# A late row block rectified by ScalarE, an input sum one step later, indirect stores through two views

## The chip, the cores and the metric

One core of a Trainium2 chip runs the whole program. Five engines work side by side, each through its own queue of instructions in a fixed order: TensorE (PE, with its weight loads as PEld), VectorE (DVE), ScalarE (ACT), GpSimd (POOL) and SyncE (SP, which only issues transfers here). An instruction waits at the head of its engine's queue until what it needs is done, and everything behind it in that queue waits too. The metric is device time of one execution in microseconds.

## The reference

An attention with decay over blocks of 64 rows feeds a Fourier mixing block with a feed-forward layer. Cut to what matters:

```python
# q, k, v: (4, 8, 768, 64); lam: (8,)
for b in range(nb):                                   # blocks of 64 rows
    intra = einsum('bhic,bhjc->bhij', qb, kb) * Dmask
    out[:, :, sl] = einsum('bhij,bhjd->bhid', intra, vb) + einsum('bhid,bhde->bhie', qb * lam_pow, kv_state)
    kv_state = lam ** 64 * kv_state + einsum('bhsd,bhse->bhde', kb * rev_pow, vb)
x = out.transpose(0, 2, 1, 3).reshape(4, 768, 512)

u = x + real(fft(fft(x, axis=1), axis=2))
un = (u - mean(u)) / sqrt(var(u) + 1e-6)              # over the last axis
return u + maximum(un @ w_ch1, 0.0) @ w_ch2           # w_ch1 512 x 2048, w_ch2 2048 x 512
```

All of it is float32. The change lies in the last line, the feed-forward layer, and in the writing of its result.

## The kernel before

**Stages.** The first part of the program computes attention, the transforms and the normalisation, batch by batch, and weaves the feed-forward layer of the first row groups into it. A row group is 256 rows of a batch; there are twelve. The first four (`PLAIN`) are multiplied plainly (`mlp`). The other eight (`LATE`) wait in DRAM and are done at the end, from 409 us of the profile on, as four pairs of groups.

**A pair.** The two matrix products of a pair are done by a scheme of seven products of half-size blocks in place of eight, with sums of blocks before and after (`PRODUCTS` lists the seven: a11·b11, a12·b21, s3·t3, s2·t2, s1·t1, a22·t4, s4·b22; a is of the weights, b of the inputs, s and t are sums). Before the pairs begin, `combine_weights` makes the sums of the weights. Most products are split once more into seven (`seven`, `deep_first`, `deep_second`). The first layer of the first pair alone is split only once: that is `first_layer(0)`. After it come the first pair's second layer and the other three pairs; `in_step` interleaves the last products of one pair with the first ones of the next, so the beginning of pair j+1 runs beside the end of pair j.

**`first_layer`.** It runs over eight blocks i of 128 hidden units. Each has seven products of four matmul instructions each (line 1031), gathered in three banks of PSUM, X, Y and Z:

- `begin(i)`: a11·b11 into X, copied out by ScalarE (line 1052); a12·b21 into Y, added by VectorE (line 1054) and rectified by it (line 1055). This runs up to three blocks ahead.
- the loop: s2·t2 is added into X, and ScalarE copies it to a12 (line 1069); s3·t3 goes into Z; s1·t1 is added into X, ScalarE copies it to a22 (line 1072), VectorE adds Z (line 1073) and rectifies (line 1074).
- `finish` of the block before, called "late" below: s4·b22 is added into X, and ScalarE rectifies that into a21 (line 1041); a22·t4 is added into Z, VectorE adds it to a12 (line 1043) and rectifies a12 (line 1044); then VectorE forms the sums a21 + a22 and a11 - a21 for the second layer (lines 1045 and 1046).

The engines' queues don't follow the text of the code exactly: a scheduler sets their order, apart from instructions pinned by `keep_in_program_order`. In VectorE's queue a late block's lines come as 1045, 1046, 1043, 1044, and the rectified a12 is read only by the second layer. Meanwhile GpSimd forms 28 sums of the second layer's weights, four for each of seven products (`keep_sums`, lines 855 and 859), and SP stores three of each four in DRAM.

**`inputs`.** For pairs 1 to 3 this generator makes the sums of the inputs that the deep first layer needs. It starts with line 941 (B12 = B22 - B12, pinned in program order), which reads what `load_u` (line 894, issued by SP) brings in. `in_step` takes a step of it in turn with a step of the products around it; each `yield` ends a step. On VectorE these sums lie among the additions of the second layer of the pair before (line 1206).

**`store`.** Results of the upper half of a batch's rows come out in reversed order, so they are written by an indirect transfer that GpSimd issues (line 738), with row numbers from the table `ix`. The lower half is written by SP (line 736). `dram_disjoint_views` tells the framework that two views of the output don't overlap, so that it orders no write in one after a write in the other; writes through one view are ordered one after another, each waiting for the one before to land.

Of the kernel before, what the change touches and what calls it, by code (L numbers as in the profile page):

```python
# [16 lines left out]
AF = mybir.ActivationFunctionType  # L17
ALU = mybir.AluOpType
# [59 lines left out]
def kernel(  # L78
# [10 lines left out]
    nc = tc.nc  # L89
# [50 lines left out]
    def new(pool, shape, tag, **kw):  # L140
        cnt[0] += 1
        return pool.tile(shape, F32, tag=tag, name=f"{tag}{cnt[0]}", **kw)
# [43 lines left out]
    def row_of(j, n=128):  # L186
        return bass.IndirectOffsetOnAxis(ap=ix[0:n, j:j + 1], axis=0)
# [540 lines left out]
    ORDER = [(b, g) for b in range(B) for g in (1, 2, 0)]  # L728
    PLAIN, LATE = ORDER[:4], ORDER[4:]

    out_low, out_high = dram_disjoint_views(out.rearrange("b s d -> (b s) d"), 2)

    def store(b, T, y, cols=slice(0, DM)):
        if T < HC:
            row = S * b + 128 * T
            nc.sync.dma_start(out_low[row:row + 128, cols], y[:, cols])
        else:
            nc.gpsimd.indirect_dma_start(out=out_high,
                                         out_offset=row_of(2 + HC * (b + 1) + T - HC),
                                         in_=y[:, :], in_offset=None)  # L740

# [67 lines left out]
    V = nc.vector  # L809
# [41 lines left out]
    def keep_sums(k):  # L851

        pin = tc.keep_in_program_order
        B11, B12, B21, B22 = quarters_b(s2.B[PRODUCTS[k][1]])
        pin(nc.gpsimd.tensor_tensor(B12, B22, B12, op=SUB))
        T1, T2, T4 = t = [new(s2.yp, [128, HF // 2, HM // 2], "tx", bufs=6) for _ in range(3)]
        s2.td.append([dram.tile([128, HF // 2, HM // 2], F32, name=f"td{k}{i}") for i in range(3)])
        for i, o, x, y, op in ((1, T2, B12, B11, ADD), (0, T1, B22, T2, SUB), (2, T4, B21, T2, SUB)):
            pin(nc.gpsimd.tensor_tensor(o, x, y, op=op))
            nc.sync.dma_start(s2.td[k][i], o)  # L860
# [37 lines left out]
    def bank():  # L898
        return new(s2.ps, [128, DM], "p2")
# [18 lines left out]
    def inputs(j):  # L918

        P, r = pairs[j], s2.u.pop(j)  # L920
        b11, b21, b12, b22 = r[:, 0, 0:2], r[:, 0, 2:4], r[:, 1, 0:2], r[:, 1, 2:4]

        def sx(shape):
            return new(s2.hp, shape, "sx", bufs=6)

        P.U = U = dict(b11=b11, b21=b21, b22=b22, t3=b12)
        if j < DEEP:
            U["t1"], U["t2"], U["t4"] = t1, t2, t4 = [sx([128, 2, G * 128]) for _ in range(3)]
            V.tensor_tensor(t1, b12, b11, op=SUB)
            yield 0.0  # L930
            V.tensor_tensor(t2, b22, t1, op=SUB)
            yield 0.0
            V.tensor_tensor(t4, b21, t2, op=SUB)
            yield 0.0
            V.tensor_tensor(b12, b22, b12, op=SUB)
            yield 0.0
            return


        B11, B12, B21, B22 = (r[:, :, k::2, m:m + 128] for k in range(2) for m in (0, 128))  # L940
        tc.keep_in_program_order(V.tensor_tensor(B12, B22, B12, op=SUB))
        yield 0.0
        t1 = U["t1"] = sx([128, 2, G * 128])
        V.tensor_tensor(t1, b12, b11, op=SUB)
        yield 0.0
        V.tensor_tensor(b12, b22, b12, op=SUB)
        yield 0.0
        T2, T1, T4 = [sx([128, 2, 2, 128]) for _ in range(3)]
        V.tensor_tensor(T2, B12, B11, op=ADD)
        yield 0.0  # L950
        V.tensor_tensor(T1, B22, T2, op=SUB)
        yield 0.0
        V.tensor_tensor(T4, B21, T2, op=SUB)
        yield 0.0
        P.T = {n: [t[:, h, k] for t in (T1, T2, T4)]
               for n, h, k in (("b11", 0, 0), ("b21", 0, 1), ("t3", 1, 0), ("b22", 1, 1))}
        t2, t4 = U["t2"], U["t4"] = [sx([128, 2, G * 128]) for _ in range(2)]
        V.tensor_tensor(t2, b22, t1, op=SUB)
        yield 0.0
        q2, q1, q4 = [new(s2.hp, [128, 3, 128], "sv", bufs=3) for _ in range(3)]  # L960
        for i, n in enumerate(("t2", "t1", "t4")):
            C11, C12, C21, C22 = (U[n][:, k, m:m + 128] for k in range(2) for m in (0, 128))
            if n == "t4":
                nc.gpsimd.tensor_tensor(t4, b21, t2, op=SUB)
                yield 0.0
            nc.gpsimd.tensor_tensor(q2[:, i], C12, C11, op=ADD)
            nc.gpsimd.tensor_tensor(q1[:, i], C22, q2[:, i], op=SUB)
            nc.gpsimd.tensor_tensor(q4[:, i], C21, q2[:, i], op=SUB)
            P.T[n] = [q1[:, i], q2[:, i], q4[:, i]]
            yield 0.0  # L970
# [10 lines left out]
    def load_x(j):  # L981
        P = pairs[j]
        P.us = [new(s2.yp, [128, G, DM], "u2", bufs=2) for _ in range(2)]
        for k in range(2):
            for s in range(G):
                tc.keep_in_program_order(nc.sync.dma_start(P.us[k][:, s], ud[P.who[k][s]]))

    def open_y(j):
        P = pairs[j]
        P.yt = new(s2.yp, [128, 2, G, DM], "y2")  # L990
        P.y = [P.yt[:, k, :, m:m + HM] for k in range(2) for m in (0, HM)]

    def split(t):

        A11, _, A21, _ = quarters_a(t)
        tc.keep_in_program_order(V.tensor_tensor(A21, A11, A21, op=SUB))
# [20 lines left out]
    def prepare_b(j, k):  # L1017
        t = yield from load_three(k, s2.td)
        pairs[j].pre_b[k] = [x.rearrange("p (a b) -> p a b", a=HF // 2) for x in t]
# [4 lines left out]
    def first_layer(j):  # L1024

        P = pairs[j]
        h, U = P.h, P.U

        def prod(ps, a, b, i, first):
            for kt in range(2):  # L1030
                nc.tensor.matmul(ps, lhsT=s2.A[a][:, kt, 128 * i:128 * i + 128], rhs=U[b][:, kt, :],  # L1031
                                 start=(first and kt == 0), stop=(kt == 1), skip_group_check=True)

        def two(t):
            return t.rearrange("p (s k) -> p s k", s=G)

        def finish(i, X, Z):
            a11, a12, a22, s1, s3 = (h[n][:, :, i, :] for n in ("a11", "a12", "a22", "s1", "s3"))
            prod(X, "s4", "b22", i, False)
            a21 = new(s2.hp, [128, G, 128], "sv", bufs=3)  # L1040
            nc.scalar.activation(a21, two(X), AF.Relu)
            prod(Z, "a22", "t4", i, False)
            V.tensor_tensor(a12, two(Z), a12, op=ADD)
            V.tensor_scalar(a12, a12, 0.0, None, op0=ALU.max)
            V.tensor_tensor(s1, a21, a22, op=ADD)
            V.tensor_tensor(s3, a11, a21, op=SUB)

        def begin(i):
            a11 = h["a11"][:, :, i, :]
            X, Y = (bank()[:, 0:G * 128] for _ in range(2))  # L1050
            prod(X, "a11", "b11", i, True)
            nc.scalar.copy(a11, two(X))
            prod(Y, "a12", "b21", i, True)
            V.tensor_tensor(a11, two(Y), a11, op=ADD)
            V.tensor_scalar(a11, a11, 0.0, None, op0=ALU.max)
            return X

        last = None
        AHEAD = 3
        begun = [begin(i) for i in range(AHEAD)]  # L1060
        for i in range(HF):
            a12, a22 = (h[n][:, :, i, :] for n in ("a12", "a22"))
            if i >= AHEAD:
                begun.append(begin(i))
            X, Z = begun[i], bank()[:, 0:G * 128]
            if last:
                finish(*last)
            prod(X, "s2", "t2", i, False)
            nc.scalar.copy(a12, two(X))
            prod(Z, "s3", "t3", i, True)  # L1070
            prod(X, "s1", "t1", i, False)
            nc.scalar.copy(a22, two(X))
            V.tensor_tensor(a22, two(Z), a22, op=ADD)
            V.tensor_scalar(a22, a22, 0.0, None, op0=ALU.max)
            last = (i, X, Z)
            if i < len(PRODUCTS):
                if i == 0:
                    tc.keep_in_program_order(nc.gpsimd.tensor_copy(s2.begun, h["a11"][:, 0, 0, 0:1]))
                keep_sums(i)
            if i == HF - 3:  # L1080
                load_x(j)
            if i == HF - 2:
                for k in range(2):
                    run(prepare_b(j, k))
            if i > HF // 2:
                split(h[("a11", "a12", "s3")[i - HF // 2 - 1]])
        run(prepare_a(j, 0))
        finish(*last)
        run(prepare_a(j, 1))
        open_y(j)  # L1090
# [263 lines left out]
    def run(gen):  # L1354
        return sum(gen)
# [82 lines left out]
```

## Time and profile before

| What | us |
|---|---|
| median of 3 runs | 777.26 |
| lowest and highest run | 775.27, 777.77 |
| profiled execution, its own time | 773.78 |
| its span in the profile | 771.7 |
| stage of `first_layer`, from its first to its last matmul | 409.6 to 461 |
| pairs from there to the last matmul | 461 to 767 |

| Stretch, us | PE busy | VectorE busy | ScalarE busy | GpSimd busy |
|---|---|---|---|---|
| 409 to 420 (11) | 10.97 | 8.54 | 2.62 | 6.50 |
| 440 to 450 (10) | 10.00 | 9.82 | 2.36 | 9.76 |
| 450 to 460 (10) | 10.00 | 9.76 | 2.63 | 3.30 |
| 460 to 498 (38) | 38.00 | 32.72 | 4.25 | 8.99 |
| 498 to 546 (48) | 47.43 | 42.75 | 16.55 | 12.96 |
| 722 to 771.7 (49.7) | 44.86 | 35.42 | 5.88 | 8.31 |

A row of a timeline gives start and length in us, engine, line, operation, the tile written and the tiles read, and in brackets how long the engine stood idle before it and for whom. Tile names are cut to letters: `p` is a bank of PSUM, `ha` stands for a11, a12 and a22, `hs` for s1 and s3, `sv` for a21, `sx`, `tx` and `ur` for inputs and their sums. One row can hold several instructions (x4). An instruction that has to wait for more than a queue's own order often shows as a longer duration, not as idle time: an operation of VectorE on 128x256 elements has a median of 0.91 us at line 1044 and a least value of 0.29.

### The profile page before, as it was taken

Reading aid. Unit: us, or ns where it says so; the run is one execution under the profiler, and the core shown is the slowest. Engines: PE = TensorE matmul, PEld = TensorE weight load, DVE = VectorE, ACT = ScalarE, POOL = GpSimd, SP = SyncE. Lnnn points to the kernel's source line nnn. Section 1 sums busy time; section 2 is a strip of 40 time slices with the busy share of each in tenths; the row PEclk is TensorE's granted clock in tenths of the full one; section 3 lists DMA queues with packets and bytes.
Section 4 is the critical chain, followed back from the end, with each engine's and each line's share of the span. In section 5 each row is a group of like instructions: output and inputs, shape, how many; then the busy total and the mean of one; then the engine's idle time right before and its main releaser. Section 6 shows DMA issues by size and latency. Waiting matters only on the chain.

```text
span 771.7 us, 15006 instructions
## 1 busy us (share of the span) xinstructions
PE 752.6 (98%) x5784; PEld 646.7 (84%) x5784; DVE 602.8 (78%) x1167; ACT 231.1 (30%) x532; POOL 178.4 (23%) x202
## 2 busy tenths in 40 slices
PE   6989999999999999999999999999999999999997
PEld 5777877777685967769747899999999999999997
DVE  6999998784936575336898999788986699758984
ACT  3755443435521221322101221034301341024310
POOL 3223330021111113220105941360015001230013
PEclk9999999999999999999999999999999999999999
DMA  9979732347943149731433465876545456455442
GB/s 240 274 161 250 195 125 86 106 96 181 246 117 94 45 82 270 176 97 35 113 65 124 150 218 164 273 234 202 180 124 178 125 186 182 127 175 180 144 141 70
DMA packets 154924, 120.22 MB, mean 156 GB/s; under 512 B 114286, under 2 KB 116974, under 8 KB 154854
## 3 DMA queue, kind: packets, MB, share of 16 engines
q1 hardware_dynamic: 147792, 100.51, 46.7%
q0 software_dynamic: 4032, 12.99, 4.7%
q10 hardware_dynamic: 3030, 5.78, 2.1%
q8 instruction: 46, 0.75, 0.4%
q14 instruction: 24, 0.20, 0.1%
HBM read 88.04 MB, written 31.20 MB: 155 GB/s over the span
## 4 chain that ended last, share of the span: by engine, by line
PE 88%; DVE 7%; DMA 2%; ACT 1%; issue 1%; POOL 0%; SPq 0%; DVEq 0%; ACTq 0%
PE p L1198 22%; PE p L1124 17%; PE pm L763 13%; PE pm L749 13%; PE p L1031 6%; PE pa L603 3%; PE pa L379 3%; PE pa L338 3%; PE pa L373 2%; PE pa L314 1%; PE pa L358 1%; PE pa L395 1%; DVE sc L343 1%; PE pa L763 1%; PE pa L319 1%
## 5 line engine op out<-in xcount | busy, mean ns | idle before, releaser
L749 PE MATMUL pm<-ut,w 128*128 128x256 f32 x512 | 118.3, 381 | 0.0
L763 PE MATMUL pm<-w,hr 128*128 128x512 f32 x240 | 108.7, 596 | 0.1
L749 PEld LDWEIGHTS pm<-ut,w 128*128 128x128 f32 x512 | 94.7, 190 | 14.4 <-issue 2.7
L763 PEld LDWEIGHTS pm<-w,hr 128*128 128x128 f32 x240 | 43.8, 190 | 45.5 <-issue 43.8
L1219 POOL TENSOR_TENSOR y<-y,u 128x512 f32<-128x512 f32 x12 | 19.9, 1661 | 186.8 <-DVE y L1228 155.5
L1198 PE MATMUL p<-tx,sx 128*128 128x128 f32 x400 | 52.7, 275 | 0.0
L1198 PEld LDWEIGHTS p<-tx,sx 128*128 128x128 f32 x400 | 48.6, 192 | 0.0
L1133 DVE TENSOR_TENSOR ha<-p,ha 128x512 f32<-128x512 f32 x60 | 40.1, 686 | 8.6 <-PE p L1124 8.6
L1204 ACT COPY y<-p 128x128 f32<-128x128 f32 x48 | 12.8, 266 | 103.6 <-PE p L1198 103.1
L310 POOL TENSOR_TENSOR kd<-k,decay 128x512 f32<-128x512 f32 x20 | 21.7, 1083 | 86.5 <-PE pa L358 50.1
L343 DVE TENSOR_TENSOR sc<-pa,decay 128x512 f32<-128x512 f32 x48 | 30.9, 683 | 11.7 <-PE pa L338 11.5
L1206 DVE TENSOR_TENSOR y<-p,y 128x128 f32<-128x128 f32 x92 | 25.6, 285 | 15.6 <-PE p L1198 9.1
L1198 PE MATMUL p<-w,ha 128*128 128x128 f32 x288 | 37.4, 275 | 0.0
L1133 DVE TENSOR_TENSOR hs<-p,hs 128x512 f32<-128x512 f32 x39 | 26.2, 685 | 12.4 <-PE p L1124 12.4
L338 PEld LDWEIGHTS pa<-qT,kT 64*128 64x128 f32 x384 | 25.1, 193 | 12.2 <-ACT qT L321 6.4
L1198 PEld LDWEIGHTS p<-w,ha 128*128 128x128 f32 x288 | 34.9, 192 | 0.1
L638 POOL TENSOR_SCALAR ve<-mv 128x2 f32<-128x2 f32 x12 | 6.2, 519 | 120.0 <-DVE mv L635 120.0
L757 ACT ACTIVATE hr<-pm 128x256 f32<-128x256 f32 x44 | 16.7, 382 | 57.6 <-PE pm L749 53.7
L1124 PE MATMUL p<-sx,tx 128*128 128x128 f32 x264 | 33.9, 275 | 0.0
L338 PE MATMUL pa<-qT,kT 64*128 64x128 f32 x384 | 30.1, 292 | 2.9 <-ACT qT L321 2.9
L1124 PEld LDWEIGHTS p<-sx,tx 128*128 128x128 f32 x264 | 31.7, 192 | 0.0
L379 PE MATMUL pa<-sc,v 128*64 128x128 f32 x384 | 28.9, 282 | 1.3 <-DVE sc L343 1.0
(274 smaller groups left out, 1748.4 us busy)
## 6 DMA issues: line engine op xcount, KB each, us to landing
tx<-td SPq DMA_DIRECT2D x84, 256.0 KB, 2.9
raw<-in_moe_w_ch_dram SPq DMA_DIRECT2D x32, 512.0 KB, 4.3
tx<-sd SPq DMA_DIRECT2D x63, 256.0 KB, 2.8
k<-in_k_dram SPq DMA_DIRECT2D x24, 256.0 KB, 3.7
q<-in_q_dram SPq DMA_DIRECT2D x24, 256.0 KB, 7.0
v<-in_v_dram SPq DMA_DIRECT2D x24, 256.0 KB, 5.7
td<-tx SPq DMA_DIRECT2D x21, 256.0 KB, 2.0
ud<-x SPq DMA_DIRECT2D x16, 256.0 KB, 3.1
```

What stands on the lines that cost most here:

```text
L310: nc.gpsimd.tensor_tensor(kd, kt, kpow, op=ALU.mult)
L338: mm(pss[hi][:, hp, :], lhsT=kT[HD[hi], hp, :], rhs=qT[HD[hi], hp, :], start=True, stop=True)
L343: nc.vector.tensor_tensor(t, pss[hi], decay[:, hi::2, :], op=ALU.mult)
L379: mm(po[HD[hi], hp, :], lhsT=vt[:, 2 * hp + hi, :], rhs=sc[hi][:, hp, :], start=(c == 0 and hp == 0), stop=(hp == HP - 1), skip_group_chec ...
L603: mm = nc.tensor.matmul(ps[:, n, :], lhsT=piece(a, i, n), rhs=cs[0:rows, a, i in (2, 3), n, :], start=(a == 0), stop=(a == 1))
L749: nc.tensor.matmul(ps, lhsT=w1[:, c, 128 * fc:128 * fc + 128], rhs=ut[:, c, :], start=(c == 0), stop=(c == KO - 1))
L763: return nc.tensor.matmul(ps, lhsT=hr[(fc - f0) // 4][:, fc % 4, 128 * i:128 * i + 128], rhs=w2[:, fc, :], start=(fc == f0), stop=(fc == f ...
L1031: nc.tensor.matmul(ps, lhsT=s2.A[a][:, kt, 128 * i:128 * i + 128], rhs=U[b][:, kt, :], start=(first and kt == 0), stop=(kt == 1), skip_gro ...
L1124: nc.tensor.matmul(ps[:, 128 * i:128 * i + 128], lhsT=ab[m][0][:, 128 * i:128 * i + 128], rhs=ab[m][1], start=(start and i == 0), stop=Tru ...
L1133: V.tensor_tensor(o, p, o, op=ADD)
L1198: nc.tensor.matmul(ps[:, 0:HM // 2], lhsT=ab[m][0][i], rhs=ab[m][1][:, i, :], start=(start and i == 0), stop=(i == HF // 2 - 1), skip_grou ...
L1206: V.tensor_tensor(o, ps[:, 0:HM // 2], o, op=ADD)
```

## The change

It has three parts. The rectifying of a12 in `finish` is written as an activation of ScalarE instead of a VectorE operation; it is done for eight blocks. In `inputs`, for the pairs from the second on, a `yield` stands ahead of the first sum, so that sum is formed one step later. The output is declared as three views that don't overlap, one for SP's stores and two for the indirect stores, which use the two in turns.

```diff
-    out_low, out_high = dram_disjoint_views(out.rearrange("b s d -> (b s) d"), 2)
+    out_low, *out_high = dram_disjoint_views(out.rearrange("b s d -> (b s) d"), 3)
+    uppers = [0]
 
     def store(b, T, y, cols=slice(0, DM)):
         if T < HC:
             row = S * b + 128 * T
             nc.sync.dma_start(out_low[row:row + 128, cols], y[:, cols])
         else:
-            nc.gpsimd.indirect_dma_start(out=out_high,
+            uppers[0] += 1
+            nc.gpsimd.indirect_dma_start(out=out_high[uppers[0] % 2],
                                          out_offset=row_of(2 + HC * (b + 1) + T - HC),
                                          in_=y[:, :], in_offset=None)
...
         B11, B12, B21, B22 = (r[:, :, k::2, m:m + 128] for k in range(2) for m in (0, 128))
+        yield 0.0
         tc.keep_in_program_order(V.tensor_tensor(B12, B22, B12, op=SUB))
...
             prod(Z, "a22", "t4", i, False)
             V.tensor_tensor(a12, two(Z), a12, op=ADD)
-            V.tensor_scalar(a12, a12, 0.0, None, op0=ALU.max)
+            nc.scalar.activation(a12, a12, AF.Relu)
             V.tensor_tensor(s1, a21, a22, op=ADD)
             V.tensor_tensor(s3, a11, a21, op=SUB)
```

## The prediction

> **What bounds the kernel now.** I read the page first, for the engine that fills the span, then busy time by stretch, for where that engine has holes, then its waits, then the order of time around each hole.
>
> ```profile
> span 771.7 us, 15006 instructions
> PE 752.6 (98%) x5784; PEld 646.7 (84%) x5784; DVE 602.8 (78%) x1167; ACT 231.1 (30%) x532; POOL 178.4 (23%) x202
> ```
>
> PE is busy 98% of the span, so an edit counts only where PE stands still. Busy time by stretch (columns: stretch, length, then PE, PEld, DVE, ACT, POOL busy, granted clock, DMA share, GB/s) and PE's waits after 409 us (total, times, longest):
>
> ```profile
> 420.00:430.00 10.00, 9.24 (x43) 7.57 (x41) 9.67 (x13) 1.87 (x5) 9.69 (x8) 1.00 0.38 141
> 430.00:440.00 10.00, 10.00 (x48) 8.81 (x48) 9.82 (x15) 2.52 (x7) 9.69 (x8) 1.00 0.36 133
> ```
> ```profile
> PE p L1031 <- DVE ha L1073: 0.8, 1, 0.8
> PE p L1198 <- DVE y L1206: 0.6, 1, 0.6
> ```
>
> Between 409 us and the last matmul these two holes, 0.76 and 0.57 us, are all that an edit could give back there: 1.33 us. The clock is 1.00, so nothing is to be had from it either. The stage of the first edit (`first_layer`, 409 to 461 us) is special in another way: VectorE is 98% busy there too, and GpSimd 97%. Five starts of products on PE, and what the other engines do meanwhile (start, length):
>
> ```profile
> 435.22 1.03 PE L1031 MATMUL p<-ur,w1s 128*128 128x256 f32 x4
> 436.08 1.03 PE L1031 MATMUL p<-sx,w 128*128 128x256 f32 x4
> 436.95 1.03 PE L1031 MATMUL p<-sx,w1s 128*128 128x256 f32 x4
> 437.81 1.03 PE L1031 MATMUL p<-ur,w 128*128 128x256 f32 x4
> 438.67 1.03 PE L1031 MATMUL p<-sx,w1s 128*128 128x256 f32 x4
> ```
> ```profile
> 436.33 0.38 ACT L1041 ACTIVATE sv<-p 128x256 f32<-128x256 f32 x1 [1.40 <-PE p L1031]
> 437.60 0.41 DVE L1045 TENSOR_TENSOR hs<-sv,ha 128x256 f32<-128x256 f32 x1
> 437.60 1.53 POOL L859 TENSOR_TENSOR tx<-w2s 128x512 f32<-128x512 f32 x1
> 437.93 1.49 DVE L1046 TENSOR_TENSOR hs<-ha,sv 128x256 f32<-128x256 f32 x1
> 438.01 0.37 ACT L1069 COPY ha<-p 128x256 f32<-128x256 f32 x1 [1.29 <-PE p L1031]
> 439.34 0.41 DVE L1043 TENSOR_TENSOR ha<-p,ha 128x256 f32<-128x256 f32 x1
> 439.79 0.91 DVE L1044 TENSOR_SCALAR ha<-ha 128x256 f32<-128x256 f32 x1
> 439.74 0.37 ACT L1072 COPY ha<-p 128x256 f32<-128x256 f32 x1 [1.35 <-PE p L1031]
> ```
>
> The products are, in order, s4·b22 and a22·t4 of the late block, then s2·t2, s3·t3, s1·t1 of the current one, 0.86 us apart. L1043 adds a22·t4, which PE had issued by 436.95, but starts at 439.34: VectorE runs 2.4 us behind PE. That harms nothing, since no instruction that PE waits for stands behind L1043 closely enough. Three VectorE operations whose operands all lie in SBUF (L1044, L1046, L1074) end shortly after a GpSimd sum does: L1044 takes 0.29 us at 461.05, when GpSimd is silent, and 0.91 us here.
>
> **Edit 1, the rectifying of the late block.** It takes L1044 off VectorE, 8 times: six of 0.91 and two of 0.29 us, 6.0 us of work. It puts 8 Relu activations on ScalarE; L1041 is the same shape there, 0.38 us, so 3.1 us on an engine 25% busy. By work alone this is a relief. The wait is the matter. The Relu waits for L1043, and in ScalarE's queue it stands, from block 3 on, directly after L1041 and ahead of L1069, the copy of s2·t2. PE may add s1·t1 to that bank only after that copy. For blocks 1 and 2 it stands ahead of L1072, which s4·b22 needs. So VectorE's lateness, harmless till now, reaches PE.
>
> The Trainium skill ("ScalarE: Activation LUTs", Rules for kernel authors) says to do relu on VectorE rather than ScalarE; its reason is the rate per element. Here the rows say otherwise on the rate (0.91 against 0.38), and by the rule's reason alone the stage would lose nothing, since ScalarE has room; it is the queue order that costs.
>
> The chain from the end of s4·b22 to s1·t1, by rows: to L1041's start 0.25 (436.08 to 436.33), L1041 0.38, on to VectorE 0.04, then x, the time from L1045's start to L1043's, then L1043 0.41, on to ScalarE 0.07 (L1054 ends 442.31, L1041 starts 442.38), Relu 0.38, copy L1069 0.37, on to PE 0.05. Without x that is 1.95. PE has three products to do meanwhile, 3 x 0.86 = 2.58. So x may be 0.63. The rows of x: 0.67 and 0.68 at 456.10 and 459.92, when GpSimd had finished; 1.74 at 432.02 and 437.60 (L1046 held by one GpSimd sum); 2.65 and 2.63 at 420.18 and 425.56 (L1045 held as well). PE therefore loses 0.04, 1.1 or 2.0 us per block.
>
> Block by block. Blocks 1 and 2: the first L1043 ends at 423.24, as no L1044 precedes it; Relu to 423.69, L1072 to 424.06 (it ended at 422.50), s4·b22 starts at 424.11 instead of 422.79. L1073 then runs at 424.13 (424.11 before), so a22·t4 follows at 424.97 instead of 424.57: the old hole of 0.76 is spent in this, and 0.4 is lost. Block 2 gives 0.1 of it back: 0.3. Block 3: VectorE still has L1074, L1054 and L1055 ahead of L1045, and reaches it at 431.95, about as now (432.02), 1.1 us after a21 is ready; L1043 ends at 434.1, Relu and copy at 434.9, s1·t1 starts at 434.97 where it was due at 432.8: 2.2. Blocks 4 and 5: VectorE, lighter by L1044, is no longer late, and x decides; the rows show both kinds, so one of 2.0 and one of 1.1. Blocks 6 and 7: GpSimd, which waits for none of this, is through at 453.4 or a little earlier; L1045 of block 6 would come at 454.5 on the delayed PE: 0.1 for both. Sum: 0.3 + 2.2 + 3.1 + 0.1 = 5.7 us lost. Bounds: 1.1 for each of blocks 3 to 5 and nothing else, 3.3; 2.2, 2.0, 2.0, 2.0 (block 6 too) with 0.4 and 0.3 around them, 8.9.
>
> The skill ("SBUF — State Buffer", Who interferes with whom) holds that a VectorE operation with two SBUF inputs, or in a two-port mode, and a GpSimd operation shut each other out for a whole instruction, and that ScalarE waits on nobody. The rows above agree for VectorE; by that rule alone edit 1 frees 6 x 0.6 us of blocked time and the sum would be a gain of at most the 0.76 us hole.
>
> **Edit 2, the first input sum one step later.** L941 now stands in VectorE's queue after one more L1206.
>
> ```profile
> 498.54 0.69 DVE L941 TENSOR_TENSOR ur<-ur 128x512 f32<-128x512 f32 x1 [2.70 <-DMA ur<-utd]
> 499.15 0.28 DVE L1206 TENSOR_TENSOR y<-p,y 128x128 f32<-128x128 f32 x1
> 499.49 0.97 PEld L1198 LDWEIGHTS p<-w2s,sx 128*128 128x128 f32 x8 [0.76 <-DVE y L1206]
> ```
>
> VectorE waits 2.7 us for the transfer of the second pair's inputs, and the L1206 behind it holds PE 0.57 us. That L1206 goes ahead now. Behind L941 stand another L1206 and the sums; the first that PE takes (L949, 501.24 to 501.91) is used at 504.95, 3.0 us later, or 2.4 once PE is earlier. So -0.57; bounds -0.57 and 0 (if the next L1206 becomes the one that holds). At 585 and 671 us L941 waits for nothing: 0. No DMA is issued by it, and SP's order is the same.
>
> **Edit 3, two views.** Each indirect store no longer waits for the previous one to land, but for the one before that. The rows of this line's semaphore waits give 17 ns at the least, 43 in the middle and 3026 at the most; the one long wait runs from 761.9 us, for the last store.
>
> ```profile
> 762.11 0.98 POOL L738 DMA_INDIRECT out_dram<-y,ix  x1 [5.50 <-DVE y L1206]
> 765.63 0.97 POOL L738 DMA_INDIRECT out_dram<-y,ix  x1 [2.54 <-DVE y L1206]
> ```
>
> That wait ends near 764.9, and VectorE delivers y only at 765.40, so the store starts when it did. It lands 2.9 us later, near 768.5, while the span ends at 771.7 with SP's last stores (issued at 767.2). 0; if that cover were gone, 0.7 us off a path that doesn't end the span. GpSimd's other waits are longer than any landing.
>
> **The sum.** 5.7 - 0.57 = +5.1 us, on 773.78 us of the profiled execution (span 771.7 and 2.1 around it): 778.9. The median shown is 777.26, 3.5 above that execution; I put the change on the median: 782.4.
>
> **Rivals.** (a) *Relief wins.* In `first_layer`, if VectorE, lighter by 0.91 a block, keeps x at or under 0.63, the Relu is always ready in time; PE keeps both holes' 1.33 us: 775.9. For it: VectorE 98% busy. Against it: 0.67 even with GpSimd silent, and GpSimd is busy till 453. The point is x = 0.63. This is within 0.3% (2.3 us, what a measurement can tell from no change); beyond that no hole is left to fill. (b) *One hold per block*: 3.3 - 0.57 = +2.7: 780.0. For it: four of the six early rows of x are near 1.74. Against: block 3's queue. (c) *Two holds per block through block 6, and edit 2 gives nothing*: +8.9: 786.2. For it: the two rows with L1045 held too, and VectorE's queue in block 3. Against: GpSimd ends early. (d) *An edit that doesn't do what it says*: the second view takes a wait away that VectorE covers, so the stores start as before. I hold this to be so, and it is part of every case.
>
> **How the numbers follow.** Forecast (+3.5 to +7.5) 0.56; (b) 0.17; (c) 0.13; (a) 0.14, of which 0.03 is faster by over 0.3% (a mistake of mine in the holes) and 0.11 within it. (b) at +2.7 lies just beyond 0.3%, so 0.02 of it goes to no change. Slower 0.84, same 0.13, faster 0.03. The range runs from 778.5 (below (b), by the scatter of 1 to 2 us in the runs) to 787.3 (past (c)).
>
> **What would show it.** Right: PE waiting in 420 to 452 us for ScalarE's L1069 and L1072, some 5 us in all; ScalarE waiting for L1043 ahead of each Relu; VectorE with idle time there; L1206 no longer behind L941's wait, and PE without its hole at the start of the second pair; second-last wait of L738 gone with the same end. Wrong: PE unbroken through 420 to 450, or L1045 and L1046 near 0.4 us there; or a new hole behind L941.

## The result, and the profile after

| | median, us | lowest and highest | runs |
|---|---|---|---|
| before | 775.98 | 775.27, 777.77 | 6 |
| changed | 779.95 | 778.45, 782.08 | 6 |

The changed kernel takes 1.0049 of the time of before, 95% interval 1.003 to 1.0067: about 3.8 us slower, where +5.1 was forecast. The page of its profiled execution begins:

```profile
span 779.9 us, 15013 instructions
PE 753.6 (97%) x5784; PEld 646.5 (83%) x5784; DVE 595.8 (76%) x1159; ACT 233.2 (30%) x540; POOL 177.1 (23%) x202
```

VectorE is busy 7.0 us less than before (602.8), ScalarE 2.1 us more (231.1): the work moved as the diff says. But the two spans can't be subtracted. The first matmul of line 603, long before any of the edits, begins at 71.3 us in the profiled execution of before, at 74.7 in the changed kernel's, and between 71.7 and 76.0 in the other profiles below. So I compare stretches after it. Busy time by stretch in the changed kernel, in the stage of `first_layer` (columns as before):

```profile
430.00:440.00 10.00, 8.20 (x38) 6.69 (x37) 6.85 (x11) 2.38 (x7) 9.76 (x8) 1.00 0.38 140
440.00:450.00 10.00, 8.36 (x40) 7.02 (x39) 6.83 (x11) 2.17 (x6) 9.69 (x8) 1.00 0.38 140
```

PE was busy for all 10 us of such a stretch and now is for 8.2 to 8.4; VectorE fell from 9.8 to 6.8. All of PE's waits after 409 us that the profile lists (total, times, longest):

```profile
PE p L1034 <- ACT ha L1072: 5.2, 3, 1.8
PE p L1034 <- ACT ha L1075: 1.0, 1, 1.0
PE p L1201 <- DVE ur L949: 0.2, 1, 0.2
```

Lines 1072 and 1075 are ScalarE's two copies (1069 and 1072 before). One of the three long waits, block 4, in order of time (1044 makes a21, 1048 and 1049 are the sums, 1046 adds a22·t4, 1047 is the new Relu):

```profile
442.06 0.38 ACT L1044 ACTIVATE sv<-p 128x256 f32<-128x256 f32 x1 [1.42 <-PE p L1034]
442.15 2.67 POOL L861 TENSOR_TENSOR tx<-w2s,tx 128x512 f32<-128x512 f32 x2
442.48 1.22 DVE L1048 TENSOR_TENSOR hs<-sv,ha 128x256 f32<-128x256 f32 x1 [0.26 <-ACT sv L1044]
443.62 1.48 DVE L1049 TENSOR_TENSOR hs<-ha,sv 128x256 f32<-128x256 f32 x1
445.02 0.41 DVE L1046 TENSOR_TENSOR ha<-p,ha 128x256 f32<-128x256 f32 x1
445.47 0.42 ACT L1047 ACTIVATE ha<-ha 128x256 f32<-128x256 f32 x1 [3.02 <-DVE ha L1046]
445.79 0.35 ACT L1072 COPY ha<-p 128x256 f32<-128x256 f32 x1
446.20 1.13 PE L1034 MATMUL p<-sx,w1s 128*128 128x256 f32 x4 [1.64 <-ACT ha L1072]
```

ScalarE stands still for 3.02 us at the head of its queue, waiting for L1046; the copy that PE needs is behind it. L1046 is late because two operations of VectorE, 0.42 us each when undisturbed, take 1.22 and 1.48 beside GpSimd's sums.

At the start of the second pair, VectorE still waits for the inputs:

```profile
508.81 0.69 DVE L944 TENSOR_TENSOR ur<-ur 128x512 f32<-128x512 f32 x1 [2.39 <-DMA ur<-utd]
509.41 0.29 DVE L1209 TENSOR_TENSOR y<-p,y 128x128 f32<-128x128 f32 x1
511.64 1.16 PE L1201 MATMUL p<-tx,sx 128*128 128x128 f32 x8 [0.18 <-DVE ur L949]
513.84 1.16 PE L1201 MATMUL p<-tx,ha 128*128 128x128 f32 x8
```

L944 is L941 of before. PE's hole of 0.57 us behind this sum is gone, but two smaller ones follow, before 511.64 and 513.84: eight matmuls take 0.89 us, so 0.36 us is idle after those of 510.39 and 0.32 after those of 512.63.

The end of the program, stores first, then the closing instructions (count, least, median and longest ns, first and last start), of the changed kernel:

```profile
771.99 0.98 POOL L740 DMA_INDIRECT out_dram<-y,ix  x1 [5.49 <-DVE y L1209]
773.78 0.97 POOL L740 DMA_INDIRECT out_dram<-y,ix  x1 [0.81 <-DVE y L1209]
...
L1436 POOLq EVENT_SEMAPHORE  x4: 17/17/17, 779.1 to 779.7; - x4
L1436 POOLq DRAIN  x3: 46/102/5453, 773.5 to 779.6; - x3
L1436 SPq DRAIN  x3: 7/7/7, 779.0 to 779.3; - x3
```

and the same closing instructions of the kernel before:

```profile
L1433 POOLq EVENT_SEMAPHORE  x4: 17/17/17, 770.9 to 771.6; - x4
L1433 POOLq DRAIN  x3: 46/102/5442, 765.4 to 771.4; - x3
L1433 SPq DRAIN  x3: 7/7/7, 769.2 to 771.1; - x3
```

A drain is a closing instruction at the end of an engine's queue. Before, SP was through with its stores at 769.2, but GpSimd's drain, which stands behind its last indirect store and whose row begins at 765.4, lasted 5.44 us, to 770.8; the program closed after that. In the changed kernel the last store follows the one before by 1.79 us instead of 3.52, and GpSimd's drain and SP are through together at 779.0.

Three stretches hold everything that the edits touch. In all profiles, in us, worked out from the starts of matmuls (first matmul of `first_layer` to its last; from there to PE's long unbroken stretch in the second pair, at 506.90 in the kernel before; from the start of the last unbroken stretch, there at 725.77, to the end of the span). The 218.87 us between the second stretch and the third are the same to 0.01 in every profile.

| Kernel | `first_layer` | to the second pair | end |
|---|---|---|---|
| before | 50.33 | 46.99 | 45.97 |
| changed | 56.78 | 47.02 | 44.20 |
| e1, edit 1 alone | 56.77 | 47.10 | 45.85 |
| e2, edit 2 alone | 50.33 | 46.59 | 45.98 |
| e3, edit 3 alone | 50.32 | 47.03 | 44.31 |
| e4, late Relu, edit 3 | 49.20 | 47.51 | 44.20 |
| e5, addition first | 50.35 | 47.28 | 44.21 |
| e6, changed, GpSimd quiet | 50.46 | 47.49 | 44.19 |
| e7, last stores by SP | 50.31 | 47.29 | 44.09 |
| e8, before, GpSimd quiet | 49.87 | 47.11 | 45.86 |
| e9, late Relu, edits 2 and 3 | 49.20 | 47.37 | 44.21 |
| e10, changed again | 56.77 | 47.28 | 44.19 |
| e11, edits 1 and 2 | 56.77 | 47.05 | 45.86 |
| e12, edit 3 again | 50.34 | 47.32 | 44.31 |

Before, e3, e7 and e12 are alike up to the second pair, and yet differ by 0.3 us in the second column: smaller differences there mean nothing. The expectations below count the first stretch in other ways. Those of e1 and e4 end it at the matmul behind it, 0.2 us later. Those of e5, e6, e8, e9 and e10 end it at its last matmul that reads `ur` and `w`, before the last products and a wait that can lie between them: 47.0 us for the kernel before and 53.3 for the changed one.

Before to changed: +6.45, +0.03, -1.77, together +4.7 us, inside what the times allow (+2.3 to +5.2).

### The profile page after: what moved, and what is told of

It reads as the page before. It is cut to its first block, busy times and chain, and to the rows that moved or that the text cites. A ratio compares the mean times of both kernels' runs of the same rounds, so it can differ in the third digit from the quotient of the medians.

```text
span 779.9 us, 15013 instructions
## 1 busy us (share of the span) xinstructions
PE 753.6 (97%) x5784; PEld 646.5 (83%) x5784; DVE 595.8 (76%) x1159; ACT 233.2 (30%) x540; POOL 177.1 (23%) x202
## 3 DMA queue, kind: packets, MB, share of 16 engines
q1 hardware_dynamic: 147792, 100.51, 46.6%
## 4 chain that ended last, share of the span: by engine, by line
PE 85%; DVE 8%; DMA 3%; ACT 2%; issue 1%; POOL 0%; DVEq 0%; SPq 0%; ACTq 0%
PE p L1201 21%; PE p L1127 17%; PE pm L765 13%; PE pm L751 13%; PE p L1034 4%; PE pa L338 3%; PE pa L603 3%; PE pa L379 2%; PE pa L373 2%; PE pa L395 1%; PE pa L358 1%; PE pa L314 1%; DMA q<-in_q_dram 1%; PE pa L319 1%; DVE hs L1049 1%
## 5 line engine op out<-in xcount | busy, mean ns | idle before, releaser
L1207 ACT COPY y<-p 128x128 f32<-128x128 f32 x48 | 12.7, 265 | 103.6 <-PE p L1201 103.2
L225 ACT ACTIVATE e<-raw 128x512 bf16<-128x512 int16 x32 | 21.9, 685 | 23.5 <-DMA raw<-in_moe_w_ch_dram 18.0
```

The lines of the kernel that those rows point to most:

```text
L225: pin(nc.scalar.activation(sg, top.bitcast(I16), AF.Sign))
```

## The experiments

**One edit at a time (e1, e2, e3).** Each takes one part of the diff shown above and leaves the kernel before as it was otherwise.

> Edit 1 alone. Theory (the Relu's wait for L1043 stands in ScalarE's queue ahead of the copies that PE needs): all of the loss is here. The stage of first_layer lasts 57 us instead of 50.6, with PE waiting 1.0 us in block 1 and 1.6 to 1.8 us in each of blocks 3, 4 and 5; the median is 6 to 6.5 us above before, ratio 1.008. Rival (the loss of the whole change is spread over the three edits, or comes from the front of the program, where the changed kernel's profile is 3.4 us later than before's): under 4.5 us, ratio under 1.006.

Measured: ratio 1.0104 (1.0086 to 1.0122); `first_layer` 56.8 us, 57.0 as the expectation counts it. PE's waits are the same to the tenth as in the changed kernel:

```profile
PE p L1031 <- ACT ha L1069: 5.2, 3, 1.8
PE p L1031 <- ACT ha L1072: 1.0, 1, 1.0
PE p L1198 <- DVE y L1206: 0.7, 1, 0.7
```

So the loss is edit 1's. The time moved by 8.1 us rather than the 6.4 of the stretches; the interval begins at 6.7, and what makes the difference is open.

> Edit 2 alone. Theory from the changed kernel's profile (the hole only moves to the next L1206 behind the sums): PE's idle time at the start of the second pair stays at 0.5 to 0.7 us, and the time is as before, within 0.3 us. Rival (the prediction on record): the hole of 0.57 us is gone and the time is 0.6 us shorter. Both are within what the runs can tell by their times, so the profile decides: from the first matmul of the second layer to the long unbroken stretch of the second pair before takes 46.6 us.

Measured: ratio 1.0000 (0.9988 to 1.0012); 46.6 us to the second pair where before and the kernels like it there have 47.0 to 47.3. Neither theory in full: 0.4 us or a little more is gained, and a hole of 0.3 us stays further down, where two sums stand between two L1206 (L1207 here). With edit 1 as well (changed, e10, e11) the stretch is 47.0 to 47.3 us, beside 47.1 in e1, and nothing is left of the gain: the inputs then land later against PE (L944 starts 0.2 us after the product of 508.61, in e2 0.24 us before the same product), and the next addition is late instead.

> Edit 3 alone. Theory (the end is set by GpSimd's drain of 5.44 us, which follows its last indirect store, and that store waited for the one before to land): the last store starts about 1.8 us after the one before instead of 3.5, and the span after PE's last matmul is 3.1 us instead of 4.8: 1.7 us shorter, ratio 0.998. Rival (the prediction on record: SP's last stores set the end, and the data were not ready earlier): the last store starts when it did and nothing changes, ratio 1.000.

Measured: ratio 0.9996 (0.9979 to 1.0012), which tells neither from the other. The profile does: the last store at 766.07, 1.79 us after the one before, and the end 1.7 us shorter.

**Is it ScalarE, or the place in its queue? (e4)** The Relu is kept back and issued behind the copies of the next block:

```diff
             V.tensor_tensor(a12, two(Z), a12, op=ADD)
-            V.tensor_scalar(a12, a12, 0.0, None, op0=ALU.max)
+            unrectified.append(a12)
...
+        def rectify():
+            while unrectified:
+                tc.keep_in_program_order(nc.scalar.activation(unrectified[0], unrectified.pop(0), AF.Relu))
...
             nc.scalar.copy(a22, two(X))
+            rectify()
...
         finish(*last)
+        rectify()
```

> Edit 3, and edit 1 with the Relu put one block later in ScalarE's queue, directly after L1072, so that no copy which PE needs waits behind an L1043 that is not yet done. Theory (it is the place in the queue, not the engine, that costs): no PE waits for ScalarE from 420 to 452 us; the stage of first_layer lasts 49.7 to 50.6 us, since VectorE is lighter and the old hole of 0.76 us shrinks; with edit 3 the time is 1.7 to 2.6 us below before, ratio 0.9967 to 0.998. Rival (ScalarE's Relu itself, longer than VectorE's fast form, costs): the stage still lasts 53 us or more.

Measured: ratio 0.9973 (0.9962 to 0.9985); `first_layer` 49.2 us, 1.1 less than before. PE has no listed wait in the stage. ScalarE's Relu in block 4, 0.42 us, starts 0.26 us after the copy and waits for nothing:

```profile
438.53 0.37 ACT L1079 COPY ha<-p 128x256 f32<-128x256 f32 x1 [1.35 <-PE p L1033]
438.79 0.42 ACT L1062 ACTIVATE ha<-ha 128x256 f32<-128x256 f32 x1
439.39 0.37 ACT L1054 COPY ha<-p 128x256 f32<-128x256 f32 x1 [0.17 <-PE p L1033]
```

The same eight activations on the same engine cost 6.4 us in one place of the queue and gain 1.1 in another. Some 0.2 to 0.5 us of the gain comes back as a longer hole at the second pair (1.1 us): PE arrives there 1.1 us earlier after the stage's start, the inputs by less (PE's hole ends 89.3 us after that start, in the kernel before 89.9).

**What makes L1043 late? (e5, e6, e8)** e5 pins the two sums behind the addition in VectorE's queue:

```diff
             nc.scalar.activation(a12, a12, AF.Relu)
-            V.tensor_tensor(s1, a21, a22, op=ADD)
-            V.tensor_tensor(s3, a11, a21, op=SUB)
+            tc.keep_in_program_order(V.tensor_tensor(s1, a21, a22, op=ADD))
+            tc.keep_in_program_order(V.tensor_tensor(s3, a11, a21, op=SUB))
```

> The changed kernel with the sums of lines 1045 and 1046 pinned behind the addition of line 1043 in VectorE's queue; nothing else differs. Theory (the loss is x, the time that these two sums, held by GpSimd's, take ahead of L1043): the Relu is ready about 0.9 us sooner or more, PE waits for ScalarE no longer than 0.3 us in any of blocks 3 to 5, the stage from first to last matmul of first_layer lasts 47.0 to 48.5 us instead of the changed kernel's 53.3, and the time is 0 to 2.5 us below before. Rival (the Relu on ScalarE delays the copies wherever L1043 stands): the stage stays at 52 us or more.

Measured: ratio 0.996 (0.9941 to 0.9979); `first_layer` 50.3 us, as long as the kernel before has it, where the changed one has 56.8 (46.2 as the expectation counts it). In block 4 (1046 the addition, 1048 and 1049 the sums) the addition no longer stands behind anything that GpSimd holds:

```profile
437.31 0.33 DVE L1058 TENSOR_SCALAR ha<-ha 128x256 f32<-128x256 f32 x1
438.51 0.42 DVE L1046 TENSOR_TENSOR ha<-p,ha 128x256 f32<-128x256 f32 x1 [0.87 <-PE p L1034]
438.85 1.42 DVE L1048 TENSOR_TENSOR hs<-sv,ha 128x256 f32<-128x256 f32 x1
440.20 1.48 DVE L1049 TENSOR_TENSOR hs<-ha,sv 128x256 f32<-128x256 f32 x1
```

The sums are held as long as ever, but nobody waits for them. The old hole of 0.76 us is gone too, but in the last blocks PE still waits for the copy behind the Relu, by 0.58 us the second time, because other work of VectorE (L1015) stands ahead of the addition there:

```profile
457.50 0.69 DVE L1015 TENSOR_TENSOR sx<-sx,ha 128x512 f32<-128x512 f32 x1
458.11 0.41 DVE L1046 TENSOR_TENSOR ha<-p,ha 128x256 f32<-128x256 f32 x1
459.29 1.13 PE L1034 MATMUL p<-sx,w1s 128*128 128x256 f32 x4 [0.58 <-ACT ha L1072]
```

The expectation's count ends ahead of this wait. So e5 takes back the loss of edit 1 and no more: the Relu's place still costs where the addition is late.

e6 is the changed kernel with GpSimd's sums left out, e8 the kernel before with the same cut:

```diff
-        pin(nc.gpsimd.tensor_tensor(B12, B22, B12, op=SUB))
...
-        for i, o, x, y, op in ((1, T2, B12, B11, ADD), (0, T1, B22, T2, SUB), (2, T4, B21, T2, SUB)):
-            pin(nc.gpsimd.tensor_tensor(o, x, y, op=op))
+        for i, o in ((1, B11), (0, B22), (2, B21)):
             nc.sync.dma_start(s2.td[k][i], o)
```

> The changed kernel without GpSimd's 28 sums of the second layer's weights; unsummed quarters are stored in their place, so the second layer multiplies other numbers. Theory (GpSimd's sums hold the operations of lines 1045 and 1046 and so set the size of the loss): L1046 takes 0.42 us, x is 0.67 to 0.75, PE waits at most 0.2 us in a block, the stage lasts 46.5 to 48 us. Rival (VectorE is late for reasons of its own): PE waits over 1 us in blocks 3 to 5 as in the changed kernel, the stage lasts 52 us or more.

> The kernel before without GpSimd's 28 sums, as the control of the quiet run: unsummed quarters are stored in their place, so the second layer multiplies other numbers. Theory: without GpSimd it makes no difference whether VectorE or ScalarE rectifies; the stage of first_layer lasts 46.0 to 47.0 us here and there, and line 1044 takes 0.29 us in all eight blocks. Rival: the quiet changed kernel's stage is longer than this one's by over 1 us.

Measured: 50.5 and 49.9 us (47.0 and 46.6 as the expectations count), from one execution each. In e6 the sums take 0.43 and 0.42 us, x is 0.68, and the profile lists no wait of PE for ScalarE, though the Relu (L1045 there) stands where it does in the changed kernel:

```profile
438.06 0.43 DVE L1046 TENSOR_TENSOR hs<-sv,ha 128x256 f32<-128x256 f32 x1 [0.51 <-ACT sv L1042]
438.40 0.42 DVE L1047 TENSOR_TENSOR hs<-ha,sv 128x256 f32<-128x256 f32 x1
438.74 0.42 DVE L1044 TENSOR_TENSOR ha<-p,ha 128x256 f32<-128x256 f32 x1
```

In e8 the rectifying takes 0.29 us in all eight blocks. Without GpSimd's sums the edit makes 0.6 us, with them 6.4. Of the 0.6, 0.3 lies in a new wait at the start of the stage, 1.04 us in e6 and 0.77 in e8, for an addition of VectorE (line 798 of before); the changed kernel and the one before don't list it.

**What ends the program? (e7, e10, e11, e12)** In e7 SP issues the last two stores of upper rows, plainly:

```diff
+            if tail:
+                row = S * b + 128 * T
+                return nc.sync.dma_start(out_high[row:row + 128, :], y[:, :])
             nc.gpsimd.indirect_dma_start(out=out_high,
```

> The kernel before, with the last two stores of upper row blocks issued by SP as plain stores, so these two blocks' rows lie in unreversed order and at other places. Theory (GpSimd's drain after its last indirect store ends the program): that drain is over long before the end, SP's stores end it, and the time from the start of the last unbroken stretch of PE to the end of the span is 44.0 to 44.4 us instead of 45.9, as with two views. Rival (the two views help in some other way, or the end is a fixed cost after the last store): it stays at 45.9.

Measured: ratio 0.9973 (0.9959 to 0.9988), the end 44.1 us. GpSimd's longest drain is 6.96 us here, but starts at 758.8 and is over at 765.7; SP sets the end at 773.9. GpSimd's last instructions are a sum and the drain:

```profile
759.93 1.71 POOL L1222 TENSOR_TENSOR y<-y,u 128x512 f32<-128x512 f32 x1
L1436 POOLq DRAIN  x3: 46/102/6960, 758.8 to 774.5; - x3
```

With one view, and with no indirect store late, the end is as early as with two views.

> The changed kernel itself, beside the next run on one chip. Theory (loss of 6.3 us in first_layer, gain of 1.7 us at the end, nearly nothing from edit 2): 4.8 us above before, ratio 1.006, and 1.5 to 1.9 us below the same kernel without the two views. Rival (the two views bring nothing in time, as their first run alone suggested): the two kernels agree within 0.5 us.

> Edits 1 and 2 without the two views. Theory: the span after the start of PE's last unbroken stretch is 45.9 us instead of 44.2, ratio to before 1.0080 to 1.0085. Rival: the ratio is that of the changed kernel, within 0.0007.

> Edit 3 alone once more, since its first run left the time open (ratio 0.9996, interval 0.9979 to 1.0012, where the profile's end is 1.7 us shorter). Theory: ratio 0.9978, with an interval that holds it. Rival (something in the front of the program takes the gain back): ratio 0.9995 or above and a front, up to the first matmul of first_layer, 1 us or more later than before's 409.6 us.

Measured: e10 ratio 1.0073 (1.0056 to 1.0091), e11 1.0078 (1.0064 to 1.0092), e12 0.9987 (0.9973 to 1.0001). The ends in the profiles agree with the theory (44.2, 45.9, 44.3 us). The times lean to it weakly: medians of 782.42 and 783.28 us are 0.9 us apart instead of 1.5 to 1.9, with intervals that overlap, and e12 lies 0.7 us below before. By the times alone the views' gain is not shown; it rests on the profiles. A later front is no answer to it: e12's 412.6 us is later than before's 409.6, but e11's, with one view, is 413.6.

**The version that beats both (e9)** is e4 with edit 2.

> The Relu one block later in ScalarE's queue, and edits 2 and 3. By the profiles so far: the stage of first_layer 1.1 us shorter than before's 47.0, the hole at the start of the second pair smaller by 0.2 to 0.6 us, the end 1.7 us earlier: together 3.0 to 3.4 us below before, ratio 0.9957 to 0.9962, which beats both kernels. If edit 2 gives nothing here, the time is that of the run without it, ratio 0.9973.

Measured: ratio 0.9954 (0.9939 to 0.9969), 773.53 us beside 777.72 for the kernel before. The stretches give 1.13 - 0.38 + 1.76 = 2.5 us of gain, below the 3.0 to 3.4 expected, because the second pair is no earlier, and near the lower end of what the times give (2.4 to 4.7). A hole of 0.5 us is left at the second pair.

## Why the prediction was right, and where it was not

**Edit 1, the direction and the mechanism: right.** The Relu's wait for L1043, its place ahead of L1069 and L1072, and x set by GpSimd's sums are each shown: by e4 (same engine, other place, no loss), by e5 (x out of the chain, the loss taken back) and by e6 with e8 (x at 0.68, 0.6 us in place of 6.4).

The Trainium skill ("SBUF — State Buffer", Who interferes with whom) has VectorE's operations with two SBUF inputs and GpSimd's operations shut each other out for a whole instruction. These runs agree: 0.42 us in e6, 1.2 to 1.5 us beside GpSimd. Its rule that relu belongs on VectorE ("ScalarE: Activation LUTs", Rules for kernel authors) would have avoided the loss here, but e4 shows that ScalarE serves as well or better where its queue allows it.

**Edit 1, block by block: one term mis-sized.** The forecast was 5.7, the stage grew by 6.45. The starts of products account for all of it. Undisturbed, they lie 0.86 us apart, so two products should take 1.73; in block 4 they take 447.17 - 443.53 = 3.64, and 1.91 is lost:

```profile
443.53 1.03 PE L1034 MATMUL p<-ur,w 128*128 128x256 f32 x4
447.17 1.03 PE L1034 MATMUL p<-ur,w 128*128 128x256 f32 x4
```

| Blocks | forecast, us | measured, us |
|---|---|---|
| 1 and 2 | 0.3 | 0.24 |
| 3 | 2.2 | 2.07 |
| 4 and 5 | 2.0 and 1.1 | 1.91 and 2.00 |
| 6 and 7 | 0.1 | 0.22 |
| sum | 5.7 | 6.45 |

"One of 2.0 and one of 1.1" was a guess between two kinds, and the term that was mis-sized: both blocks were of the long kind, with x of 2.54 and 2.64. The rule x - 0.63 gives 1.91 and 2.01 for them, which is what was lost. In block 3, L1048 started at 435.33, 1.1 us after a21, with x = 1.74, as said. That the chain came out so well has some luck in it: the Relu takes 0.416 us, not L1041's 0.38, but the copy behind it starts 0.1 us before the Relu's end.

The listed waits (1.80, 1.64 and 1.74 in blocks 3 to 5) are 0.27 us smaller than these losses. A single matmul's row lasts 0.38 us and the next one starts 0.22 after its start, so the first 0.16 of a wait isn't listed as idle, and the product after a wait takes 0.97 us in place of 0.86. For this reason "all that an edit could give back: 1.33 us" was too low as well: in e4 the stage gained 1.1 us where 0.76 was listed. And "VectorE is 98% busy there too, and GpSimd 97%" holds from 420 to 450 us only, not for the whole stage.

**Edit 2: mis-sized.** -0.57 was taken from bounds of -0.57 and 0. Alone it gave about -0.4, with edit 1 nothing that can be told from 0. The step that failed is "the next L1206 becomes the one that holds", which I gave to the bound and not to the sum.

**Edit 3: wrong.** Two steps failed. "VectorE delivers y only at 765.40" took the releaser that the profile infers for the data's arrival. The rows with two views show the store start at 773.78, 0.28 us after the addition of 773.21 ends; the same addition in the kernel before ended at 763.6, so the store stood ready for 1.3 us until the one before had landed at 764.9, and began 0.7 us after that:

```profile
763.32 0.29 DVE L1206 TENSOR_TENSOR y<-p,y 128x128 f32<-128x128 f32 x1 [0.60 <-PE p L1198]
773.21 0.29 DVE L1209 TENSOR_TENSOR y<-p,y 128x128 f32<-128x128 f32 x1 [0.60 <-PE p L1201]
```

And "the span ends with SP's last stores" overlooked the closing instructions: GpSimd's drain ended it. The gain of 1.7 us or so at the end is in all nine profiles with the last indirect store early or gone, and in none of the other five.

**The sum.** +5.1 forecast; +4.7 by the stretches; +4.0 by the medians. That it came so close is luck in part: the forecast lies 0.75 us too low for edit 1, 0.6 too low for edit 2 and 1.8 too high for edit 3, and these errors mostly cancel.

**The rivals.** (a), relief wins, did not happen, but e4 shows that it was there to be had: 1.1 us in the stage. Its point of decision held: in e6, with x of 0.68, PE loses 0.05 us in each of blocks 4 to 6. (b), one hold per block, fits none of the losses in blocks 3 to 5; (c), two holds and nothing from edit 2, fits them, but block 6 was not held. (d), held to be so in every case, is refuted: with two views the last store starts 1.79 us after the one before, not 3.52.

## What to carry to other kernels

Before an operation is moved to an engine with room, look at what it waits for and at what stands behind it in the new queue: eight short activations cost 6.4 us ahead of two copies and gained 1.1 behind them. Then look at what is late on the engine it waits for: lateness that harms nobody becomes a loss as soon as another queue waits on it. And read the closing instructions: the last transfer to be issued is not always what ends a program.

## What was not expected of the hardware

GpSimd drains behind its last instruction before the program can close. In the 13 profiles that end with an indirect store the drain lasts 5.44 to 5.45 us and ends 4.24 us after the store's row, while the store's data land 2.8 to 2.9 us after issue; so the program ends more than 5 us after that store is issued. The drain doesn't need a store: in e7 it ends 4.10 us after GpSimd's last sum, and some 75 us after the last indirect store was issued. An indirect store that waits for another begins 0.7 us after that one has landed, one that waits for VectorE 0.3 us after the addition.
